# Fused linear attention and squared-ReLU MLP on one core: batch 1's second and batch 2's first matrix multiplication in the plain form, the weights' block sums moved, tail numerators of two batches alternating, and a new table of shifts

## The chip, the core and the metric

The kernel runs on one core of one Trainium2 chip. The core's engines work side by side: TensorE (PE; its weight loads are shown apart as PEld), VectorE (DVE), ScalarE (ACT), GpSimd (POOL) and SyncE (SP), which here only issues transfers. DMA engines move data between HBM and the on-chip memory (SBUF); PE writes to eight PSUM banks. The metric is the time of one execution on the device in microseconds, lower is better. It is given as the median of several runs.

## The reference

Eight batches of eight heads, 576 positions, 64 channels: linear attention with cosine weights, whose output is the input of an MLP with squared ReLU (4608 tokens, width 512, hidden width 2048). Cut to what is computed:

```python
batch, n_heads, seq, head_dim = (8, 8, 576, 64)
n_tokens, d_model, d_ff = (4608, 512, 2048)

theta = np.pi / 2.0 * pos / S
cos_w, sin_w = np.cos(theta), np.sin(theta)
def phi(x, c, s):
    r = np.maximum(x, 0.0)
    return np.concatenate([r * c, r * s], axis=-1)
q_p, k_p = phi(q, cos_w, sin_w), phi(k, cos_w, sin_w)
kv = np.einsum('bhsf,bhsd->bhfd', k_p, v)
z = np.sum(k_p, axis=2)
num = np.einsum('bhsf,bhfd->bhsd', q_p, kv)
den = np.einsum('bhsf,bhf->bhs', q_p, z)[..., None] + 1e-06
x = (num / den).transpose(0, 2, 1, 3).reshape(B * S, H * D)

h = x @ w_in
r = np.maximum(h, 0.0)
g = r * r
out = g @ w_out
```

## The kernel before

**Blocks of tokens.** The 576 positions of a batch are four pieces of 128 and a tail of 64. The MLP works on blocks m of 512 tokens: block m below 8 is the four pieces of batch m, block 8 is the eight tails. Matrices are in bf16, sums in f32.

**Attention of a batch.** k and q are turned into features (`feat`, L321 on ACT and L325 on DVE: ReLU times the cosine or the sine), v is cast beside a column of ones (`att_v`, L343), PE makes kv and z (`att_kv`, L367), and they are copied out (`att_kvz`, L378). The features of q are transposed, from batch 2 on by a DMA (`att_qT`, L391). PE multiplies them with kv (`att_num`, L418), DVE divides by the last column (`att_div`, L436, L439 and L442), and the result x is transposed by a DMA (`att_x`, L459) into xT. Tails of two batches b and b + 1 lie on the two halves of the 128 partitions and go through `att_num` together, batch b's eight matmuls and then batch b + 1's.

**Two forms of a matrix multiplication.** The plain form of the first one (`unit_mm`, L503) takes 64 matmuls with 512 columns, one unit of four for each of 16 blocks of hidden channels; ACT applies the ReLU (L512), DVE squares (`square`, L520). The seven-product form works on a 2 x 2 split of each matrix and needs seven block products for eight, with sums of blocks before and after them:

- first multiplication (`in_product`, L580; planned by `plan_gemm1_7`): four sums of x blocks (`x_sum`, L562), four sums of weight blocks made once (`w1_sum`, L538), and for each of four units seven products of four matmuls with 256 columns. ACT copies one product aside (L976), copies banks into banks to start other sums from them (`seed`, L959) and applies the ReLU to two of four blocks (L596). DVE adds the other two (`in_add`, L603), applies their ReLU (`in_max`, L620) and squares (L520).
- second multiplication (`product`, L748; planned by `plan_gemm2`): eight sums of activation blocks for each m (`g_sum`, L727), eight sums of weight blocks made once (`w2_sum`, L708), seven products of 16 matmuls with 256 columns. ACT seeds (L1027), copies (L1037, L1050), DVE adds (L1033).

Block 0 uses the plain form in both multiplications (`first_mm`, L628, and `first_out`, L653). Block 1's first multiplication is plain; its second, and both of blocks 2 to 8, have seven products. `FIRST_7 = 2` in L1202 is the first block whose first multiplication has seven.

**What sets the order.** After the head of batch 0 all work is put into a planner (`Plan`, L58). Each operation has an engine (or a choice between ACT and DVE, `add_either`), a duration, the tiles it reads and writes, and sometimes a due time. `Plan.order` propagates due times backwards, adds to each operation's due time an entry of the table `SHIFTS` (its key is the operation's number), and lists the operations by a simulated start. `Plan.run` then writes out the instructions in that order: each engine and each queue executes its own in order. Every change of the list of operations renumbers them, and so takes another table. `win[m]` is the stretch of plan time in which the second multiplication of block m, the first of block m + 1 and the attention of batch m + 2 lie side by side.

**The lines around the change.** The weight sums of w_out are entered in L1191 to L1197 with an earliest time (`after=tB + 8`); those of w_in by `plan_w1_sums` in L1233. The activation sums are entered by `plan_gemm1` (L912 to L915) when the plain form makes g, and by `plan_gemm1_7` (L998) otherwise. The result is stored from two buffers `ysb` (`put`, L674).

Of the kernel before, what the change touches and what calls it, by code (L numbers as in the profile page):

```python
# [17 lines left out]


SHIFTS = {  # L20
# [34 lines left out]
}  # L55


# [95 lines left out]
def kernel(  # L153
# [9 lines left out]
    nc = tc.nc  # L163
    P = nc.NUM_PARTITIONS
# [5 lines left out]
    HB = DFF // P  # L170
# [53 lines left out]
    def rows(b):  # L224
        return slice(b % 2 * TAIL, (b % 2 + 1) * TAIL)
# [185 lines left out]

    def att_num(b, j, num=NUM):
        qpT = qpTs[b, j]
        for b2 in (b,) if j < J else (b, b + 1):
            ps = ALL if j < J else rows(b2)
            for hh in range(HH):
                for half in range(2):
                    nc.tensor.matmul(  # L418
                        out=num[half][ps, hh * E1 : (hh + 1) * E1],
                        lhsT=qpT[half][:, hh, ps],  # L420
                        rhs=kvzs[b2][:, half * HH + hh, :],
                        start=True,
                        stop=True,
                    )
# [226 lines left out]
    def first_out(hb):  # L651
        for tt in range(J):
# [5 lines left out]
                stop=(hb == HB - 1),  # L658
            )

    def y_of(m, i):
        if (m, i) not in ys:
            ys[m, i] = home(mlp, [P, 2, DM], "ysb", i, F32)
        return ys[m, i]
# [55 lines left out]
    def g_sum(m, n, h0, h1):  # L720
        in0, in1 = {
            1: (g_block(m, 1, 0), g_block(m, 1, 1)),
            2: (gs_of(m, 1), g_block(m, 0, 0)),
            3: (g_block(m, 0, 0), g_block(m, 1, 0)),
            4: (g_block(m, 0, 1), gs_of(m, 2)),
        }[n]
        nc.vector.tensor_tensor(  # L727
            out=gs_of(m, n)[:, h0:h1, :],
            in0=in0[:, h0:h1, :],
            in1=in1[:, h0:h1, :],  # L730
            op=ALU.add if n == 1 else ALU.subtract,
        )
# [133 lines left out]

    def plan_num(b, j, due):
        r = [where[b, j], ("kvz", b % 3)] + ([("kvz", (b + 1) % 3)] if j == J else [])
        add("PE", 0.27 if j < J else 0.54, lambda: att_num(b, j), r=r, w=[("T",)], due=due)
        add("DVE", 1.05, lambda: att_div(b, j), r=[("T",)], w=[x_key(j)])  # L870

    def plan_x(b, i):
# [29 lines left out]
    def plan_gemm1(m, t, dt, banks, plain=False):  # L902
        order = list(range(HB)) if plain else [hb for h in range(HB2) for hb in (h, h + HB2)]
        for n, hb in enumerate(order):
            plan_unit(m, hb, banks[n % len(banks)], t + n * dt, halves=plain and n < 3)
            u = n // 4
            k = 2 if plain and u == 3 else 4
            if n % k == k - 1:
                a = n % 4 + 1 - k
                add("DVE", 0.06 + 512 * k * 0.00053, lambda u=u, a=a, k=k: square(m, u, plain, a, k),  # L910
                    w=[key for x in order[n + 1 - k : n + 1] for i in range(2) for key in g_keys(m, i, x // HB2, (x % HB2,))])
            if n % 4 == 3:  # L912
                if u >= 2 if plain else u % 2:
                    c = u - 2 if plain else u // 2
                    plan_g_sums(m, 4 * c, 4 * c + 4)  # L915

    def plan_w1_sums(after):
        first, second = [("w1", 0), ("w1", 1)], [("w1", 2), ("w1", 3)]
# [81 lines left out]
    def plan_g_sums(m, h0, h1):  # L1000
        hs = range(h0, h1)
        g = lambda i, j: g_keys(m, i, j, hs)
        s = lambda n: [("gs", n, h) for h in hs]
        dur = 0.06 + 256 * (h1 - h0) * 0.00053
        for n, r, w in (
            (1, g(1, 0) + g(1, 1), s(1)),
            (2, s(1) + g(0, 0), s(2)),
            (3, g(0, 0) + g(1, 0), g(1, 0)),
            (4, g(0, 1) + s(2), s(4)),
        ):  # L1010
            add("DVE", dur, lambda n=n: g_sum(m, n, h0, h1), r=r, w=w)

    def plan_gemm2(m, t, dt):
        hs = range(HB2)
# [170 lines left out]
    for tt in range(J):  # L1185
# [2 lines left out]
            r=[("bank", FIRST_Y[tt])], w=[("y", tt // 2, tt % 2)])  # L1188
        if tt % 2:
            add("SP", 1.5, lambda tt=tt: put(0, tt // 2, nc.sync), r=[("y", tt // 2, 0), ("y", tt // 2, 1)], w=[("out", 0, tt)], lag=3.5)  # L1190
    for n in range(1, 5):  # L1191
        for c in range(2):
            p = {1: 5, 2: 6, 3: 7, 4: 4}[n]
            before = {1: [], 2: [("w2t", 5, c)], 3: [], 4: [("w2t", 6, c)]}[n]
            add("DVE", 0.60, lambda n=n, c=c: w2_sum(n, 4 * c, 4 * c + 4),
                r=before + ([("w2", 2 + c)] if n == 3 else [("w2", c), ("w2", 2 + c)]),
                w=[("w2t", p, c)] + ([("w2", c)] if n == 3 else []), after=tB + 8)  # L1197
    win = {}
    t = tB + 4.0
    dC = 0.98  # L1200
    win[0] = (t, t + 14.0)
    FIRST_7, STRIDE, SHIFT = 2, 2.0, -6.0  # L1202
    if FIRST_7 == 1:
        plan_w1_sums(28.0)
        plan_gemm1_7(1, t, 0.5)
# [11 lines left out]
    for b in range(2, B):  # L1217
# [13 lines left out]
        t0, t1 = win[m - 1]  # L1231
        if m == FIRST_7:
            plan_w1_sums(28.0 if m == 2 else win[m - 2][0])  # L1233
        plan_gemm2(m - 1, t0, (t1 - t0) / 14)
        if m < FIRST_7:
            plan_gemm1(m, t0, (t1 - t0) / HB, (2, 0, 1, 3))
        else:
# [88 lines left out]
```

## Time and profile before

| | us |
|---|---|
| median of 3 runs | 279.09 (278.84 to 279.17) |
| the profiled execution | 279.47 |
| its span (first to last instruction) | 277.7 |
| PE busy in the span | 266.2 (96%) |
| PEld busy | 220.3 (79%) |
| DVE busy | 228.6 (82%) |
| ACT busy | 190.3 (69%) |

The span is what the profile shows; the rest of the profiled execution's time lies around it. PE is not busy only at the beginning (before the first loads have landed), in two stretches between 70 and 100 us, and at the end (the last copies and stores). The chain that ended last runs through PE for 83% of the span, through waits for DMAs for 5%, and through DVE and ACT for 4% each. The granted clock of PE was 0.998.

How to read the views used below: a group's row gives line, engine, operation, what is written and read, count, then busy time and mean duration of one, then the idle time of the engine before these instructions and what ended it. In a row of a timeline or of the chain of waits the first number is the start and the second the length. A matmul's duration includes its way through the array (273 ns for 256 columns), while matmuls follow each other at 109 ns.

### The profile page before, as it was taken

To read this page: it belongs to the slowest core of one execution; us is meant where nothing else is said; L and a number is where in the kernel's file an instruction comes from. 1 tells how busy PE (TensorE), PEld (TensorE's weight loads), DVE (VectorE), ACT (ScalarE), POOL (GpSimd) and SP (SyncE) were. 2 spreads that over 40 slices of the span, in tenths; PEclk is the share of its full clock that TensorE was granted. 3 is DMA by queue.
4 is the path that set the end of the run, shared out by engine and by line. 5 is a ranking of instruction groups with operands and counts; after the bars stand their busy time and mean duration, and the time that the engine had idled before them with its cause. 6 is when DMAs were issued, how large, how long until landed. Compare 5 with 4: busy or idle time off the path is not lost.

```text
span 277.7 us, 6808 instructions
## 1 busy us (share of the span) xinstructions
PE 266.2 (96%) x2755; PEld 220.3 (79%) x2755; DVE 228.6 (82%) x452; ACT 190.3 (69%) x342; POOL 19.2 (7%) x33
## 2 busy tenths in 40 slices
PE   8899999999799979999999999999999999999993
PEld 2478955565589869899899898998988888888882
DVE  1677896889999989899999986999999977697900
ACT  3575862596998989579957996998454563647231
POOL 8427000000000000000000000000000000000023
PEclk9999999999999999999999999999999999999999
DMA  7999999899989999998989599989122200300134
GB/s 211 317 206 289 309 242 316 255 222 346 206 230 240 272 230 190 315 315 151 249 263 306 144 254 243 273 164 218 38 41 84 88 0 2 151 4 0 78 113 113
DMA packets 83470, 53.38 MB, mean 192 GB/s; under 512 B 55888, under 2 KB 79824, under 8 KB 83440
## 3 DMA queue, kind: packets, MB, share of 16 engines
q1 hardware_dynamic: 77312, 42.28, 60.2%
q0 software_dynamic: 6048, 10.62, 16.2%
q8 instruction: 21, 0.34, 0.5%
q10 hardware_dynamic: 80, 0.07, 0.1%
q14 instruction: 9, 0.07, 0.1%
HBM read 36.70 MB, written 9.44 MB: 166 GB/s over the span
## 4 chain that ended last, share of the span: by engine, by line
PE 83%; DMA 5%; DVE 4%; ACT 4%; POOL 1%; issue 1%; POOLq 0%; ACTq 0%; DVEq 0%
PE bank L748 33%; PE bank L580 30%; PE bank L628 4%; PE bank L653 4%; PE bank L503 3%; PE abank L367 3%; PE abank L418 3%; DMA q<-in_q_dram 3%; DMA xT<-x 3%; PE bank L400 1%; ACT qp L321 1%; ACT kp L321 1%; DVE x L442 1%; DVE qp L325 1%; DVE kp L325 1%
## 5 line engine op out<-in xcount | busy, mean ns | idle before, releaser
L748 PEld LDWEIGHTS <-gT 128*128 128x128 bf16 x512 | 49.6, 98 | 6.2
L596 ACT ACTIVATE gT<-bank 128x512 bf16<-128x512 f32 x56 | 33.3, 602 | 26.2 <-PE bank L580 26.1
L580 PE MATMUL bank<-xT,w1sb 128*128 128x256 bf16 x336 | 48.6, 273 | 1.7 <-DMA xT<-x 1.5
L580 PEld LDWEIGHTS <-w1sb 128*128 128x128 bf16 x448 | 43.0, 98 | 7.2 <-DMA xT<-x 1.7
L748 PE MATMUL bank<-w2sb,gT 128*128 128x256 bf16 x384 | 48.0, 273 | 0.0
L603 DVE TENSOR_TENSOR gT<-bank,qpTp 128x512 bf16<-128x512 f32 x56 | 36.3, 684 | 8.6 <-PE bank L580 7.9
L748 PEld LDWEIGHTS <-gs 128*128 128x128 bf16 x384 | 36.8, 98 | 6.7 <-DVE gs L727 2.4
L520 DVE TENSOR_TENSOR gT<-gT 128x2048 bf16<-128x2048 bf16 (+1 forms) x32 | 37.7, 1185 | 1.4 <-ACT gT L596 1.1
L959 ACT COPY bank<-bank 128x512 f32<-128x512 f32 x56 | 31.8, 584 | 5.1 <-PE bank L580 4.3
L580 PEld LDWEIGHTS <-w1t 128*128 128x128 bf16 x336 | 32.0, 98 | 3.6
L748 PE MATMUL bank<-w2t,gs 128*128 128x256 bf16 x256 | 32.4, 273 | 1.9 <-DVE gs L727 1.9
L580 PE MATMUL bank<-qpTp,w1t 128*128 128x256 bf16 x224 | 32.5, 273 | 0.0
L442 DVE TENSOR_TENSOR x<-abank,rden 128x512 bf16<-128x512 f32 x31 | 21.4, 691 | 1.1
L976 ACT COPY qpTp<-bank 128x512 f32<-128x512 f32 x28 | 15.9, 590 | 8.6 <-PE bank L580 7.8
L682 POOL DMA_DIRECT2D out_dram<-ysb x4 | 2.4, 614 | 241.3 <-ACT ysb L1037 238.9
L1033 DVE TENSOR_TENSOR ysb<-bank,y 128x512 f32<-128x512 f32 x16 | 11.0, 687 | 9.3 <-PE bank L748 8.4
L580 PE MATMUL bank<-xT,w1t 128*128 128x256 bf16 x112 | 16.6, 273 | 0.0
L321 ACT ACTIVATE kp<-k,sin_col 128x512 bf16<-128x512 f32 x22 | 15.5, 720 | 1.5 <-DMA k<-in_k_dram 1.5
L580 PE MATMUL bank<-zeros,w1sb 128*128 128x256 bf16 x112 | 16.3, 273 | 0.0
L748 PE MATMUL bank<-w2t,gT 128*128 128x256 bf16 x128 | 16.1, 273 | 0.0
L748 PE MATMUL bank<-w2sb,gs 128*128 128x256 bf16 x128 | 16.1, 273 | 0.0
L628 PE MATMUL bank<-xT,w1sb 128*128 128x256 bf16 (+1 forms) x160 | 15.2, 251 | 0.0
(104 smaller groups left out, 413.7 us busy)
## 6 DMA issues: line engine op xcount, KB each, us to landing
out_dram<-ysb SPq DMA_DIRECT2D x16, 512.0 KB, 3.3
v<-in_v_dram SPq DMA_DIRECT2D x12, 512.0 KB, 5.3
q<-in_q_dram SPq DMA_DIRECT2D x12, 512.0 KB, 6.3
k<-in_k_dram SPq DMA_DIRECT2D x12, 512.0 KB, 6.9
v<-in_v_dram POOLq DMA_DIRECT2D x2, 1024.0 KB, 12.4
w1sb<-in_moe_w_in_dram POOLq DMA_DIRECT2D x4, 512.0 KB, 12.7
w2sb<-in_moe_w_out_dram POOLq DMA_DIRECT2D x4, 512.0 KB, 15.1
k<-in_k_dram SPq DMA_DIRECT2D x1, 1024.0 KB, 5.3
```

Of the source, the lines that this page charges most:

```text
L321: eng.activation(out=dst[ps, :, lo : lo + D], in_=src[ps], func=ACTF.Relu, scale=col[ps])
L442: nc.vector.tensor_tensor(out=x[:, a:z], in0=n4[:, :, :, 0:D].rearrange("p b (k l) d -> p b k l d", l=2), in1=rden[:, a:z] .rearrange("p b ...
L520: nc.vector.tensor_tensor(out=g, in0=g, in1=g, op=ALU.mult)
L580: nc.tensor.matmul(out=bank[to][:, s * W : (s + 1) * W], lhsT=lhs[:, kb, (2 * u + s) * P : (2 * u + s + 1) * P], rhs=rhs[:, kb, :], start= ...
L596: nc.scalar.activation(out=g_pair(m, i, j, u), in_=bank[to][:, :].rearrange("p (s c) -> p s c", s=2), func=ACTF.Relu,)
L603: nc.vector.tensor_tensor(out=g_pair(m, i, j, u), in0=bank[to][:, :].rearrange("p (s c) -> p s c", s=2), in1=in_five(u).rearrange("p (s c) ...
L628: nc.tensor.matmul(out=bank[2 * (s % 2) + i // 2][:, i % 2 * W + c : i % 2 * W + c + step], lhsT=w1sb[:, kb, hb * P : (hb + 1) * P], rhs=x ...
L653: nc.tensor.matmul(out=bank[FIRST_Y[tt]][:, :], lhsT=gT_of(0)[:, hb, tt * P : (tt + 1) * P], rhs=w2sb[:, hb, :], start=(hb == 0), stop=(hb ...
L748: nc.tensor.matmul(out=bank[to][:, s * DM2 : (s + 1) * DM2], lhsT=lhs[:, hb, s * P : (s + 1) * P], rhs=rhs[:, hb, :], start=(fresh and hb ...
L959: add("ACT", psum, lambda: nc.scalar.copy(out=bank[b][:, :], in_=bank[a][:, :]), r=[("bank", a)], w=[("bank", b)])
L976: add("ACT", psum, lambda u=u, Y=Y: nc.scalar.copy(out=in_five(u), in_=bank[Y][:, :]), r=[("bank", Y)], w=five)
L1033: lambda: nc.vector.tensor_tensor(out=y_view(m, i, cc), in0=half_bank(a), in1=five_of(m)[:, :, :], op=ALU.add),
```

## The change

Four things change, besides the table:

1. `FIRST_7` goes from 2 to 3: block 2's first multiplication takes the plain form (`unit_mm`), and the weight sums of w_in are entered for block 3.
2. Block 1's second multiplication takes the plain form, in a new function: 64 matmuls with 512 columns into banks 4 and 5, two groups of 128 tokens at a time, copied out by ACT and DVE. `plan_gemm1` no longer enters activation sums for block 1.
3. The weight sums of w_out are entered behind it, without an earliest time.
4. `att_num` of the tails changes its loops: the two batches' matmuls alternate. The planner's duration for it goes from 0.54 to 0.36.

```diff
 SHIFTS = {
-    40: -2.8, 60: -2, 72: -3.8, 74: -2.4, 78: 4, 92: -1.2, 126: -1.4, 137: 1.2, 145: 7.4, 147: 2.2,
...
+    24: 2.4, 27: 4.4, 38: 2, 45: -2, 70: 2.6, 72: -12, 103: 8.6, 108: -11.2, 111: -8.8, 124: 1.2,
...
 }
...
     def att_num(b, j, num=NUM):
         qpT = qpTs[b, j]
-        for b2 in (b,) if j < J else (b, b + 1):
-            ps = ALL if j < J else rows(b2)
-            for hh in range(HH):
-                for half in range(2):
+        parts = ((b, ALL),) if j < J else ((b, rows(b)), (b + 1, rows(b + 1)))
+        for hh in range(HH):
+            for half in range(2):
+
+                for b2, ps in parts:
                     nc.tensor.matmul(
                         out=num[half][ps, hh * E1 : (hh + 1) * E1],
...
+    LAST_Y = (4, 5)
+
+    def out_pair(m, i, hbs):
+        for hb in hbs:
+            for s_ in range(2):
+                tt = 2 * i + s_
+                nc.tensor.matmul(
+                    out=bank[LAST_Y[s_]][:, :],
+                    lhsT=gT_of(m)[:, hb, tt * P : (tt + 1) * P],
+                    rhs=w2sb[:, hb, :],
+                    start=(hb == 0),
+                    stop=(hb == HB - 1),
+                )
+
+    def pair_copy(m, i, s_, eng):
+        copy = eng.copy if eng is nc.scalar else eng.tensor_copy
+        copy(out=y_of(m, i)[:, s_, :], in_=bank[LAST_Y[s_]][:, :])
...
-        add("PE", 0.27 if j < J else 0.54, lambda: att_num(b, j), r=r, w=[("T",)], due=due)
+        add("PE", 0.27 if j < J else 0.36, lambda: att_num(b, j), r=r, w=[("T",)], due=due)
...
             if n % 4 == 3:
-                if u >= 2 if plain else u % 2:
-                    c = u - 2 if plain else u // 2
-                    plan_g_sums(m, 4 * c, 4 * c + 4)
+                if not plain and u % 2:
+                    plan_g_sums(m, 4 * (u // 2), 4 * (u // 2) + 4)
...
+    def plan_gemm2_plain(m, t, dt):
+        order = list(range(HB))
+        for i in range(2):
+            for n in range(0, HB, 2):
+                hbs = order[n : n + 2]
+                add("PE", 4 * 0.2158, lambda i=i, hbs=hbs: out_pair(m, i, hbs), r=[("w2", hbs[0] // 4)]
+                    + [key for hb in hbs for key in g_keys(m, i, hb // HB2, (hb % HB2,))],
+                    w=[("bank", x) for x in LAST_Y], due=t + (i * HB + n) / 2 * dt, name=f"o{m}.{i}.{n}")
+            for s_ in range(2):
+                e = ("ACT", "DVE")[s_]
+                add(e, cost(e, 512, "psum"), lambda s_=s_, e=e, i=i: pair_copy(m, i, s_, ENG[e]),
+                    r=[("bank", LAST_Y[s_])], w=[("y", i, s_)])
+            add("SP", 1.5, lambda i=i: put(m, i, nc.sync), r=[("y", i, 0), ("y", i, 1)], w=[("out", m, i)], lag=3.5)
...
-    for n in range(1, 5):
-        for c in range(2):
-            p = {1: 5, 2: 6, 3: 7, 4: 4}[n]
...
-                w=[("w2t", p, c)] + ([("w2", c)] if n == 3 else []), after=tB + 8)
+    def plan_w2_sums():
+        for n in range(1, 5):
+            for c in range(2):
+                p = {1: 5, 2: 6, 3: 7, 4: 4}[n]
...
+                    w=[("w2t", p, c)] + ([("w2", c)] if n == 3 else []))
...
-    FIRST_7, STRIDE, SHIFT = 2, 2.0, -6.0
+    FIRST_7, STRIDE, SHIFT = 3, 2.0, -6.0
...
-        plan_gemm2(m - 1, t0, (t1 - t0) / 14)
+        if m == 2:
+            plan_gemm2_plain(1, t0, (t1 - t0) / 16)
+            plan_w2_sums()
+        else:
+            plan_gemm2(m - 1, t0, (t1 - t0) / 14)
```

The rest of `SHIFTS` is replaced in the same way. `win` depends on `FIRST_7` too: the stretch of block 1 becomes 1.6 us of plan time longer.

More of the change, by code (lines that the diff above doesn't have):

```diff
@@ L1190 @@
             add("SP", 1.5, lambda tt=tt: put(0, tt // 2, nc.sync), r=[("y", tt // 2, 0), ("y", tt // 2, 1)], w=[("out", 0, tt)], lag=3.5)
-    for n in range(1, 5):
-        for c in range(2):
-            p = {1: 5, 2: 6, 3: 7, 4: 4}[n]
-            before = {1: [], 2: [("w2t", 5, c)], 3: [], 4: [("w2t", 6, c)]}[n]
-            add("DVE", 0.60, lambda n=n, c=c: w2_sum(n, 4 * c, 4 * c + 4),
-                r=before + ([("w2", 2 + c)] if n == 3 else [("w2", c), ("w2", 2 + c)]),
-                w=[("w2t", p, c)] + ([("w2", c)] if n == 3 else []), after=tB + 8)
+    def plan_w2_sums():
+        for n in range(1, 5):
+            for c in range(2):
+                p = {1: 5, 2: 6, 3: 7, 4: 4}[n]
+                before = {1: [], 2: [("w2t", 5, c)], 3: [], 4: [("w2t", 6, c)]}[n]
+                add("DVE", 0.60, lambda n=n, c=c: w2_sum(n, 4 * c, 4 * c + 4),
+                    r=before + ([("w2", 2 + c)] if n == 3 else [("w2", c), ("w2", 2 + c)]),
+                    w=[("w2t", p, c)] + ([("w2", c)] if n == 3 else []))
     win = {}
```

65 rows, old and new, of the table SHIFTS are left out of this document.

## The prediction

> **What bounds the kernel now.** I read the table of ten-microsecond stretches first, because an average over the whole span hides stages. Its columns are the stretch, then busy time (and instructions) of PE, PEld, DVE, ACT and POOL, granted clock, DMA share, GB/s.
>
> ```profile
> 60.00:70.00 10.00, 10.00 (x77) 5.20 (x76) 8.82 (x19) 6.96 (x14) 0.00 (x0) 1.00 1.06 303
> 70.00:80.00 10.00, 7.87 (x75) 5.78 (x73) 9.90 (x21) 10.00 (x18) 0.00 (x0) 1.00 0.97 230
> 80.00:90.00 10.00, 10.00 (x133) 8.91 (x131) 9.90 (x21) 8.88 (x18) 0.00 (x0) 1.00 1.06 234
> 90.00:100.00 10.00, 8.54 (x91) 7.48 (x89) 9.83 (x20) 9.79 (x18) 0.00 (x0) 1.00 1.14 263
> 130.00:140.00 10.00, 10.00 (x121) 9.02 (x119) 9.96 (x21) 9.49 (x18) 0.00 (x0) 1.00 1.07 212
> ```
>
> Nearly everywhere the matrix engine has no idle time: what counts is the number of matmul columns. The exception is 70 to 100 us, where DVE and ACT are full together and PE stands for 2.13 and 1.46 us. At 130 to 140 DVE is as full and PE loses nothing. So a full DVE alone is no stall; a backlog on it is. That stretch is batch 1's second matmul together with batch 2's first, what the change rewrites. The waits (who waits <- for whom: total, times, longest), the timeline there and the chain that ended last:
>
> ```profile
> PE bank L748 <- DVE gs L727: 1.9, 1, 1.9
> PE bank L580 <- DMA xT<-x: 1.5, 1, 1.5
> ```
>
> ```profile
> 74.55 1.29 DVE L727 TENSOR_TENSOR gs<-gT 128x1024 bf16<-128x1024 bf16 x2
> 75.30 1.21 PE L748 MATMUL bank<-w2t,gs 128*128 128x256 bf16 x8 [1.89 <-DVE gs L727]
> 90.06 0.69 DVE L442 TENSOR_TENSOR x<-abank,rden 128x512 bf16<-128x512 f32 x1
> 91.75 3.36 SPq L459 DMA_TRANSPOSE xT<-x  x1
> ```
>
> ```profile
> 65.00 1.73 PE bank L503 x8
> ...
> 91.75 7.08 DMA xT<-x
> ...
> 259.89 12.24 PE bank L748 x112
> ```
>
> The first wait is for batch 1's activation sums (L727), work that only the seven-product form has. The second is batch 3's x: divided at 90.75 (90.06 + 0.69), its transpose issued at 91.75 behind a load on SP, landed at 98.83, while PE was there at about 97.2. A wait is counted from the modelled end of the last matmul, 273 ns after its start, where matmuls follow at 109 ns; each costs 0.16 us more than its row. With ACT's 0.25 us at 78.9 and a second gs wait (0.16) the stretch loses 1.89 + 1.46 + 0.25 + 3 x 0.16 + 0.16 = 4.2 us.
>
> **The change part by part.** *PE, added.* A seven-product multiplication is 112 matmuls of 256 columns: 12.24 us by the chain's last row. The plain one is 64 of 512; L503's eight take 1.73, so 13.84. Two are exchanged: +3.2 us. In a stretch where PE never waits this goes straight to the end.
>
> *DVE and ACT, removed.* DVE loses for batch 1 eight L727 (0.69 us each) and for batch 2 eight L603 (0.65), four L562 and four L620 (0.42 each): 14.1 us of busy time; two L1033 become two copies of the same length. The planner then hands DVE five more features (0.48) and four fewer casts (0.42). Net 13 us less. ACT: per unit two relus, two seeds and a copy (about 0.59 each), 20 in all, 11.9 us, become 16 relus at 0.61, 9.7; of L1050, L1027 and L1037 five copies become two, 1.8 less; five features fewer and four casts more, 1.1 less: 5 us less. None of this is on PE's path by itself; it is what the 4.2 us waited for.
>
> *Where the backlog goes.* I took both programs' order of instructions, cut it into stretches of 10 us of matmul work from batch 0's first L628, and summed DVE and ACT in each at their back-to-back time (the second L727 above adds 1.29 - 0.69 = 0.60). Before, the sixth stretch (about 71 to 84 us of the trace) holds 13.1 us of DVE and 12.4 of ACT against 10 of PE, and the three after it 10.3, 10.0 and 9.6 of DVE: the backlog reaches 5.1 us and nothing works it off. In the changed program that stretch holds 9.1 and 7.1, the next 4.9 and 4.4, and no stretch more than 10.6 of DVE or 10.1 of ACT. Its largest backlog is 1.9 us; the old program carries 2.1 us at its later peak (about 190 us of the trace) and PE loses nothing there. So I take both waits, and ACT's, as gone: -4.2 us. Bounds: the gs waits must go, their instructions no longer exist (-2.2); the x and seed waits may stay.
>
> *The sums moved.* By the order, three of four L538 weight sums of w_in move from before 42 us to DVE's light stretch around 72 to 77 us, and the fourth stays just behind the last plain matmul that reads its block. Of the eight L708 sums of w_out, four come earlier (among L653's matmuls, where DVE is busy 6.63 of 10 us) and four go to about 106 to 110. DVE executes in order: behind the fourth L538 (1.22) stand a square, the x sums of batch 3 and the gs of batch 2, and PE waits for those. In the 20 us of matmul work from there DVE has 20.5 us of work: cover for all but 0.5 us. SP issues the same number of transfers and transposes; no new queue is passed.
>
> *Tails.* Four times 16 matmuls of 65 columns, two batches one after the other, become alternating pairs on the two halves of the array's columns:
>
> ```profile
> 66.56 0.41 PE L418 MATMUL abank<-kvz,qpT 128*128 128x65 bf16 x8
> 77.31 0.60 PE L418 MATMUL abank<-kvz,qptT 128*64 128x65 bf16 x16
> ```
>
> Eight take 0.41 (a last latency included) and sixteen 0.60: the second eight cost 0.19, or 24 ns each. If pairs ran wholly together, 0.19 would go in each tail, 0.76 in four; if not at all, 0. Near to neither end; the second eight already go faster than the 29 ns of an ordinary one, so some overlap exists: 0.4. The Trainium skill ("TensorE: Matmul & The Clock Gate", section "Wait — 56ns, not 53.3ns?") says that matmul starts never come closer than about 25 ns however small they are. By that rule 64 matmuls could save at most 4 ns each, an estimate of 0.26 us, and the sum would be 0.1 worse; the row's 24 ns already lies at that floor, and single starts of 0 to 7 ns apart occur in the trace.
>
> *What comes late next.* The x transposes. From division to landing they took 3.0 to 8.1 us in this trace, the second of a batch (which the x sums wait for) 5.9 at most; from issue to landing the tile's view says:
>
> ```profile
> DMA to landing us min/median/max: 2.5/4.1/7.2
> ```
>
> In the changed order the division of the second pair stands 7.1 (batch 2), 6.3 (batch 3) and 5.3 us (batch 4) of matmul work ahead of its reader, the first pair 7.7 and more. Most landings fit; the tight ones I price at 0.4 us in all, bounds 0 and 2.6. The program's end (12.24 us of products, then copies and stores) is unchanged.
>
> Sum: +3.2 - 4.2 - 0.4 + 0.4 = -1.0 us. The profiled execution took 279.47 us for a span of 277.7, so 1.8 lie around it, and the median of the runs is 279.09, 0.4 below. The edits touch only the span, so I subtract from the median: **278.1 us**. With 0 for the tails it is 278.5; with all of them and no late landing, 277.3; if head waits go too (0.4 us each at 23.1 and 53.6, where DVE now has less to do), 276.5.
>
> **The rivals.** *Half is given back (same).* The stall only moves: the fourth L538 cannot start before the plain form's last reader, and batch 1's copies out of the banks must wait for batch 0's store to leave that buffer, in the trace 8.24 us at its slowest (issued at 80.13). DVE's 0.5 us without cover and such a store, another 0.6, reach PE at batch 3's product 5 or batch 2's product 5. Then 278.1 + 1.1 = 279.2. For it: 20.5 against 20 us of work. Against it: DVE comes into that stretch without backlog.
>
> *Slower: late transposes.* One mechanism: with plain units PE reaches batches 3 and 4 sooner than their x. If division to landing takes the 8.1 us of batch 3's first pair, not the 3 to 6 of the other second pairs, the three second pairs are late by 8.1 less 7.1, 6.3 and 5.3 less about 0.5 of slack in the x sums: 0.5 + 1.3 + 2.3 = 4.1, less the 0.4 already counted: 278.1 + 3.7 = 281.8; with the two later ones at 7.2 us (0.4 + 1.4, less 0.4) it is 279.5. PE begins to wait at 5.8 us, and from about 7.3 the kernel is slower than before. For it: the DMA engines' share is 1.0 to 1.1 through all these stretches. Against it: only first pairs, behind loads, took over 6.
>
> *It doesn't do what it says.* The tails give nothing, because a change of column half costs what the overlap gains, and the weight sums "later" are half earlier: 278.5.
>
> **How the numbers follow.** Forecast 0.54, given back 0.20, slower 0.20, not as said 0.06; the slower case has a fifth, though no second pair was that late, because two of the six first pairs were. The likeliest alone reaches from 277.3 to 278.6. The range starts at 276.9, where part of the head's waits go as well, and reaches into the slower case, to 280.6; outside lie most of its upper half and little below. About 0.2%, 0.56 us, can be told from no change. The forecast is faster but for a tenth, given back is mostly within, the slower case slower but for its mildest: 0.55 faster, 0.23 same, 0.22 slower.
>
> **What would show it.** Right: between 70 and 100 us PE busy 10 of 10 with DVE under 9.9; no row of PE waiting for gs; L653's kind of matmul (512 columns) 64 more in each of two lines; L418's 16 on qptT in less than 0.60. Wrong: a row of PE or DVE waiting for DMA xT of over 1 us, DVE at 9.9 in 90 to 110 with PE below 9.5, or a wait of DVE for the store of ysb. If PE is full throughout and the time is still above 279, then the two forms' price (3.2) is wrong.

## The result and the profile after

The changed kernel takes 277.5 us (median of 4 runs, 277.15 to 277.98) beside 279.03 for the kernel before on the same chip: a ratio of 0.9947, with a 95% interval of 0.9931 to 0.9963. Run again later beside three experiments it took 277.3 us, 0.9932 (0.9918 to 0.9947). So it is 1.5 to 1.8 us faster; 1.0 was forecast. The profiled execution took 277.98 us for a span of 276.2.

The ten-microsecond stretches of the changed kernel come first; columns as before the change (stretch, then busy time and instructions of PE, PEld, DVE, ACT, POOL, granted clock, DMA share, GB/s).

```profile
70.00:80.00 10.00, 9.95 (x61) 4.54 (x60) 9.90 (x20) 7.94 (x15) 0.00 (x0) 1.00 1.09 231
80.00:90.00 10.00, 9.95 (x101) 5.60 (x101) 4.82 (x13) 6.45 (x12) 0.00 (x0) 1.00 1.00 287
90.00:100.00 10.00, 9.95 (x57) 4.98 (x57) 9.06 (x16) 7.85 (x15) 0.00 (x0) 1.00 1.20 241
```

PE lost 2.13 and 1.46 us here before; now it shows 0.05 in each stretch. These are not waits: the busy table has 2651 matmuls for 2659 weight loads, and each gap of 53 ns follows a pair of starts that is exactly one usual interval of a 512-column matmul (215 ns) too far apart. A matmul record is missing there. DVE, full for 30 us before, has half a stretch to spare between 80 and 90. The list of PE's waits, from its top:

```profile
PE abank L366 <- DVE vext L342: 2.6, 1, 2.6
PE bank L348 <- DVE zeros L243: 1.2, 1, 1.2
PE bank L399 <- ACT qp L320: 0.5, 1, 0.5
PE bank L464 <- DVE x L442: 0.2, 1, 0.2
```

All of the first three lie in the program's first 15 us. The rows for gs (1.9) and for DMA xT (1.5) are gone, and so are the row for L468's xT at 53.6 us and the one for L325's kp at 57.6. The chain that ended last and the timeline of PE show what stands in their place, the plain second multiplication (L667) and a tail:

```profile
70.71 5.99 PE bank L667 x27
```

```profile
78.36 0.44 PE L418 MATMUL abank<-kvz,qptT 128*64 128x65 bf16 x16
```

The first row is from the chain that ended last: 27 matmuls without a break, where PE had stood for gs. The tail of 16 takes 0.44 us where it took 0.60.

To compare kernels whose heads differ by chance, I split each profile like this. The body runs from the first L628 matmul to the end of the last matmul. For each matmul I took the time to the next one's start, less the median of this time for its line and size; what came to 0.23 us or more is summed as waits, and the rest of the body is matmul columns and what hides among them. One kind of gap is left out of the waits: 0.32 or 0.34 us ahead of a matmul of the plain second multiplications (L653 and L667 in the changed kernel) that follows one of a tail, which the profile puts down to issue. The changed kernel's trace has 61 matmuls of L653 and 60 of L667 beside 64 weight loads of each. After the tail at 43 us the next start comes 347 ns later, where the kernel before has 122, and the difference is one 512-column interval: a record is missing there too.

| kernel | body us | waits us | rest us |
|---|---|---|---|
| before | 254.0 | 5.5 | 248.5 |
| changed (both profiles) | 251.6 | 0.7 | 250.9 |
| only the tails (e1) | 253.6 | 5.7 | 247.9 |
| tails, old forms, other order (e7) | 253.8 | 6.1 | 247.7 |
| only the second multiplication plain (e5, e9, e12) | 252.2, 251.6, 251.4 | 2.7, 2.3, 2.1 | 249.5, 249.3, 249.2 |
| only the first one plain (e6) | 251.8 | 2.4 | 249.4 |
| one plain form more (e8) | 253.0 | 0.4 | 252.6 |
| sums put back (e10) | 256.2 | 5.0 | 251.2 |

The changed kernel trades 4.8 us of waits for 2.4 us of rest. Its body is 2.4 us shorter than before, the span only 1.5: in its first profile the first L628 starts at 19.67 us (19.38 in the second), before at 18.99. Over all profiles of kernels with the changed order this start lies at 18.5 to 19.7, with the old order at 18.5 to 19.0, so whether the new table makes the head later or the loads did stays open.

### The profile page after: what moved, and what is told of

The parts are those of the page before. It is cut to its first block, busy times and chain, and to the rows that moved or that the text cites. A ratio compares the mean times of both kernels' runs of the same rounds, so it can differ in the third digit from the quotient of the medians.

```text
span 276.2 us, 6556 instructions
## 1 busy us (share of the span) xinstructions
PE 265.8 (96%) x2651; PEld 210.5 (76%) x2659; DVE 216.5 (78%) x429; ACT 186.4 (67%) x334; POOL 19.3 (7%) x33
## 4 chain that ended last, share of the span: by engine, by line
PE 89%; DMA 3%; ACT 2%; DVE 2%; POOL 1%; issue 1%; POOLq 0%
PE bank L766 31%; PE bank L580 27%; PE bank L503 9%; PE bank L653 5%; PE bank L667 5%; PE bank L628 4%; PE abank L366 3%; PE abank L418 3%; DMA q<-in_q_dram 3%; ACT qp L320 1%; PE bank L399 1%; PE bank L487 1%; ACT gT L638 1%; DVE x L442 1%; PE bank L464 0%
## 5 line engine op out<-in xcount | busy, mean ns | idle before, releaser
L766 PEld LDWEIGHTS <-gT 128*128 128x128 bf16 x448 | 43.5, 98 | 5.1
L766 PE MATMUL bank<-w2sb,gT 128*128 128x256 bf16 x336 | 42.2, 273 | 0.0
L580 PE MATMUL bank<-xT,w1sb 128*128 128x256 bf16 x288 | 41.1, 273 | 0.0
L580 PEld LDWEIGHTS <-w1sb 128*128 128x128 bf16 x384 | 36.9, 98 | 4.5
L596 ACT ACTIVATE gT<-bank 128x512 bf16<-128x512 f32 x48 | 28.8, 605 | 14.4 <-PE bank L580 14.1
L603 DVE TENSOR_TENSOR gT<-bank,qpTp 128x512 bf16<-128x512 f32 x48 | 31.0, 684 | 6.0 <-PE bank L580 5.9
L766 PEld LDWEIGHTS <-gs 128*128 128x128 bf16 x336 | 32.4, 98 | 3.7
L580 PEld LDWEIGHTS <-w1t 128*128 128x128 bf16 x288 | 27.7, 98 | 3.7
L503 PE MATMUL bank<-xT,w1sb 128*128 128x512 bf16 x116 | 27.7, 379 | 0.0
L512 ACT ACTIVATE gT<-bank 128x512 bf16<-128x512 f32 x32 | 18.6, 596 | 10.2 <-PE bank L503 10.1
L503 PEld LDWEIGHTS <-w1sb 128*128 128x128 bf16 x116 | 10.7, 98 | 11.0
L628 PE MATMUL bank<-xT,w1sb 128*128 128x256 bf16 (+1 forms) x160 | 15.4, 251 | 0.1
L436 DVE TENSOR_SCALAR den<-abank 128x8 f32<-128x8 f32 x35 | 5.6, 160 | 12.3 <-PE abank L418 12.3
```

Of the source, the lines that this page charges most:

```text
L503: nc.tensor.matmul(out=out_, lhsT=w1sb[:, kb, hb * P : (hb + 1) * P], rhs=x_block(m, kb), start=(kb == 0), stop=(kb == KB - 1),)
L512: nc.scalar.activation(out=gT_of(m)[:, hb, :], in_=bank[to][:, :], func=ACTF.Relu)
L580: nc.tensor.matmul(out=bank[to][:, s * W : (s + 1) * W], lhsT=lhs[:, kb, (2 * u + s) * P : (2 * u + s + 1) * P], rhs=rhs[:, kb, :], start= ...
L596: nc.scalar.activation(out=g_pair(m, i, j, u), in_=bank[to][:, :].rearrange("p (s c) -> p s c", s=2), func=ACTF.Relu,)
L603: nc.vector.tensor_tensor(out=g_pair(m, i, j, u), in0=bank[to][:, :].rearrange("p (s c) -> p s c", s=2), in1=in_five(u).rearrange("p (s c) ...
L628: nc.tensor.matmul(out=bank[2 * (s % 2) + i // 2][:, i % 2 * W + c : i % 2 * W + c + step], lhsT=w1sb[:, kb, hb * P : (hb + 1) * P], rhs=x ...
```

## The experiments

Ratios are to the kernel before on the same chip in the same session, with their 95% intervals.

**The tails alone (e1).** The kernel before with its old forms and order; only the loop of `att_num` is the new one.

```diff
-        for b2 in (b,) if j < J else (b, b + 1):
-            ps = ALL if j < J else rows(b2)
-            for hh in range(HH):
-                for half in range(2):
+        parts = ((b, ALL),) if j < J else ((b, rows(b)), (b + 1, rows(b + 1)))
+        for hh in range(HH):
+            for half in range(2):
+                for b2, ps in parts:
```

> The kernel before with the tails' matmuls alternating, and nothing else changed (the old table, the old order on every engine). In the trace of the changed kernel the sixteen starts of a tail span about 0.25 us, before 0.40. Theory (PE is the bound wherever a tail stands): 4 x 0.15 = 0.6 us less, 278.4. Rival (the tails' gain is lost in waits for the division that follows, or a switch of column half costs time once other work surrounds it): no change, 279.0. Rival (the tails are the larger part of the whole gain of 1.5 us): 277.9 or less.

278.0 us (277.64 to 279.8), 0.9963 (0.9932 to 0.9993). PE's two long waits, for gs and for xT, have the same rows as before (1.9 and 1.5 us). The first tail in the timeline:

```profile
76.80 0.44 PE L418 MATMUL abank<-kvz,qptT 128*64 128x65 bf16 x16
```

The stalls stay, the tail goes from 0.60 to 0.44. Four of them make 0.6 us, and the rest of the body falls by as much. The body itself is only 0.4 us shorter, because the wait for a seed at 78 us grew by 0.15. The median fell by 1.1, but the interval reaches from 0.2 to 1.9 us.

**The changed kernel with its tails in turn (e2).** The converse edit, in the changed kernel.

> The changed kernel with the tails one batch after the other again, everything else as it is. Theory: 0.6 us more than the changed kernel, 278.1, so that the two plain forms with their table keep 0.9 us. Rival (the forms bring nothing, all of the gain is the tails'): 279.0.

278.17 us, 0.9962 (0.9936 to 0.9987), and the tail again:

```profile
78.07 0.60 PE L417 MATMUL abank<-kvz,qptT 128*64 128x65 bf16 x16
```

The body is 0.7 us longer than the changed kernel's, with the same waits. So alternating gives 0.6 to 0.7 us with either order.

**Short activation sums in the kernel before (e3).**

```diff
     def g_sum(m, n, h0, h1):
+        w = 8 if m == 1 else W
...
-            out=gs_of(m, n)[:, h0:h1, :],
+            out=gs_of(m, n)[:, h0:h1, 0:w],
...
+        for n in (1, 2, 4):
+            nc.gpsimd.memset(gs_of(1, n)[:, :, :], 0.0)
```

> The kernel before with batch 1's activation sums made for 8 of their 256 columns only (the rest of the three buffers is set to zero at the start, by GpSimd, and one block of g keeps its values), so the output of batch 1 is not the reference's. DVE loses about 4.6 us of work around 74 to 95 us; PE does exactly the same matmuls in the same order. Theory (PE's waits between 70 and 100 us are one backlog on DVE): both waits go, 4.2 us, 274.8. Rival (the x wait is the DMA queue's own): the gs waits alone, 2.2 us, 276.8. Rival (the wait moves to the next thing that DVE or ACT owes): under 1 us, 278.0 or more.

Slower: 282.63 us, 1.012 (1.0076 to 1.0165). Most of it I had brought in myself. DVE's and POOL's timelines where the buffers are zeroed:

```profile
27.91 5.23 DVE L325 TENSOR_SCALAR qp<-q,sin_col 128x512 bf16<-128x512 f32 x1
```

```profile
27.54 5.31 POOL L1297 MEMSET gs<- 128x2048 bf16 x3
```

A feature that takes 0.48 us elsewhere takes 5.23 while POOL fills three buffers, and PE then stands for 2.5 us. This run can't be read by its time. What it still tells is the wait in question, in PE's and DVE's timelines:

```profile
77.15 1.05 PE L749 MATMUL bank<-w2t,gs 128*128 128x256 bf16 x8 [1.15 <-DVE gs L728]
```

```profile
74.05 1.22 DVE L520 TENSOR_TENSOR gT<-gT 128x2048 bf16<-128x2048 bf16 x1
75.19 1.22 DVE L538 TENSOR_TENSOR w1sb<-w1sb 128x2048 bf16<-128x2048 bf16 x1
76.32 0.69 DVE L520 TENSOR_TENSOR gT<-gT 128x1024 bf16<-128x1024 bf16 x1
76.92 0.30 DVE L728 TENSOR_TENSOR gs<-gT 128x32 bf16<-128x32 bf16 x2
```

Two sums in 0.30 us where the kernel before took 1.29 shorten PE's wait only from 1.89 to 1.15. The rest is what stands ahead of the sum in DVE's order: squares, and a weight sum of 1.22 us. It is the queue that is late, more than the sum. What the memsets had cost DVE was worked off by then: it begins these sums 1.1 us after PE is ready for them, before 1.3.

The theory itself (one backlog on DVE makes all these waits) failed here. Between 70 and 102 us PE still loses 4.3 us start to start: 0.35 for batch 2's xT, 1.31 for gs, 1.09 for a seed and 1.59 for batch 3's xT. The last one matters most. Its division, its transpose and PE's wait:

```profile
91.48 0.17 DVE L436 TENSOR_SCALAR den<-abank 128x8 f32<-128x8 f32 x1 [0.79 <-PE abank L418]
92.84 4.60 SPq L459 DMA_TRANSPOSE xT<-x  x1
101.21 0.61 PE L580 MATMUL bank<-xT,w1sb 128*128 128x256 bf16 x4 [1.43 <-DMA xT<-x]
```

DVE had been idle, waiting for PE, and the transpose was issued 0.2 us after the division; it landed 8.3 us later. So this wait was not made by DVE's queue, as the run's first rival had said.

**Fewer columns in the plain product (e4).** The changed kernel, `out_pair` on 448 of 512 columns.

```diff
-                    out=bank[LAST_Y[s_]][:, :],
+                    out=bank[LAST_Y[s_]][:, 0:448],
...
-                    rhs=w2sb[:, hb, :],
+                    rhs=w2sb[:, hb, 0:448],
```

> The changed kernel with batch 1's plain second multiplication made for 448 of its 512 columns, so the last 64 columns of batch 1's output are not the reference's. 64 matmuls lose 64 columns each, 27 ns at the 216 ns that 512 take: 1.7 us of matmul work, about what the seven-product form would have saved, and no other engine does less. Theory (nothing but matmul columns sets the time of the changed kernel after the head): 1.7 us less, 275.8. Rival (DVE, ACT or the transfers are just behind PE in this stretch and take over): under 0.8 us less, 276.7 or more.

276.16 us, 0.9905 (0.9874 to 0.9936): 1.3 us below the changed kernel, with an interval of about 1 us on either side. The body is 0.7 us shorter; its rest fell by 1.5, close to the columns taken out, and 0.8 us came back as new small waits, the largest this one:

```profile
PE bank L580 <- ACT bank L976: 0.4, 1, 0.4
```

So columns do set the time, but the cover is thin: a PE that is 1.5 us earlier already meets ACT.

**Half of the change: only batch 1's second multiplication plain (e5).**

```diff
-    FIRST_7, STRIDE, SHIFT = 3, 2.0, -6.0
+    FIRST_7, STRIDE, SHIFT = 2, 2.0, -6.0
```

and a table searched for its own list of operations, as in all that follow except the last two.

> The changed kernel with batch 2's first multiplication back in seven products: only batch 1's second one is plain, with an order worked out anew for this form. PE's columns cost 1.6 us more than before instead of 3.2; DVE loses the eight activation sums of batch 1 (5.5 us) but keeps batch 2's 8.6 us of input sums and bank copies. If the stalls of 70 to 100 us come from DVE's backlog of 5.1 us, 5.5 us less is just enough: waits gone as in the changed kernel, +1.6 - 4.2 - 1.0 (waits at 50 to 59) - 0.6 (tails), so 275 to 276.5 us beside 279.1. If both plain forms are needed for the relief, the x wait and the seeds' waits stay (2 us): 277 or more.

276.79 us, 0.993 (0.9903 to 0.9957), between the times of the theory and of its rival. gs and seed waits are gone; what is left is the row that the slower rival had named:

```profile
PE bank L642 <- DMA xT<-x: 1.2, 2, 0.9
```

**The other half: only batch 2's first multiplication plain (e6).**

```diff
-        if m == 2:
-            plan_gemm2_plain(1, t0, (t1 - t0) / 16)
-            plan_w2_sums()
-        else:
-            plan_gemm2(m - 1, t0, (t1 - t0) / 14)
+        if m == 2:
+            plan_w2_sums()
+        plan_gemm2(m - 1, t0, (t1 - t0) / 14)
```

(The planner enters batch 1's activation sums again as before.)

> The other half alone: batch 2's first multiplication plain, batch 1's second one in seven products with its activation sums, with an order worked out anew for this form. PE +1.6 us, DVE 8.6 us less, ACT 2.2 less. By the backlog theory 8.6 is more than the 5.1 us needed, so PE's waits for gs and xT are gone or under 0.5 together: 275 to 276.5. By the rival that the wait for gs belongs to the form itself (sums that only the seven products have, late however empty DVE is) a wait of PE for gs of 1 us or more stays: 277 to 278.

278.17 us, 0.9972 (0.9957 to 0.9987). In the timeline of PE:

```profile
73.13 1.48 PE L822 MATMUL bank<-w2t,gs 128*128 128x256 bf16 x12 [0.58 <-DVE gs L801]
```

The sums are all there, yet the wait for them fell from 1.89 to 0.58 us when other work left DVE (busy 221.8 us in all, before 228.6). That is below the 1 us that the rival (a wait that belongs to the form) asked for. The order is another one too, though, so it need not be the work alone. The time is above what either theory gave: the body is as short as the changed kernel's (251.8 us), but PE still waits 0.75 for that sum, start to start, 0.8 in all for xT and kp at 53 to 57 and 0.5 for a seed at 267 us.

**The old forms with a new order (e7).** The kernel before with alternating tails and a table searched in the same manner.

> The old forms throughout (both multiplications in seven products), with the alternating tails, and an order of the instructions searched anew in the same manner as for the two kernels with half of the change. If it was DVE's and ACT's work that had to go, no order removes the stalls: 277.7 to 278.6, like the old order with the alternating tails (278.0), with waits of 3 us or more between 70 and 100 us. If the changed kernel owes its gain to its new table of order alone, the waits are gone here too, without the 3.2 us: 274 to 275.5.

279.96 us, 1.0048 (1.0025 to 1.0072): slower than the old order. PE's and DVE's timelines:

```profile
75.28 1.03 PE L642 MATMUL bank<-qpTp,w1t 128*128 128x256 bf16 x8 [1.80 <-DVE qpTp L624]
```

```profile
72.60 0.68 DVE L789 TENSOR_TENSOR gs<-gT 128x1024 bf16<-128x1024 bf16 x1
73.21 1.28 DVE L582 TENSOR_TENSOR gT<-gT 128x1024 bf16<-128x1024 bf16 x2
74.41 0.48 DVE L387 TENSOR_SCALAR kp<-k,cos_col 128x512 bf16<-128x512 f32 x1
74.81 0.41 DVE L624 TENSOR_TENSOR qpTp<-xT 128x512 bf16<-128x512 bf16 x1
```

This order puts the sums of activations early enough, and so the sums of x come late: PE waits 1.80 us for those at 73 and 1.56 at 127. A third new one, 1.4 us for an ACT ReLU, comes at 35 us. So the waits are 6.1 us in all, but only 2.0 of them lie between 70 and 100 us, where the theory had put 3 or more. The wait for batch 3's xT is not among them. Another order chose other victims. One searched order doesn't prove that none exists, but the table alone did not make the gain here.

**One plain form more (e8).**

```diff
-    FIRST_7, STRIDE, SHIFT = 3, 2.0, -6.0
+    FIRST_7, STRIDE, SHIFT = 4, 2.0, -6.0
```

> The changed kernel with one multiplication more in the plain form: batch 3's first one, with an order worked out anew. 64 matmuls of 512 columns for 112 of 256: +1.6 us of PE where it has no wait left to lose. If PE's columns alone set the time now, 1.6 us above the changed kernel: 278.7 to 279.6 (ratio to before 0.999 to 1.002). If DVE's load still costs PE something that the waits don't show, 277.0 to 278.0.

279.08 us, 1.0 (0.9983 to 1.0017). The gain is given back, 1.6 us above the changed kernel, as its first theory said:

```profile
100.00:110.00 10.00, 10.00 (x102) 5.40 (x101) 9.86 (x18) 6.36 (x12) 0.00 (x0) 1.00 0.94 250
```

PE was full there already. ACT gets room that nobody needs (busy 176.5 us in all, in the changed kernel 186.4; DVE 215.4 and 216.5), and 1.6 us of columns go straight to the end: the rest of the body rises by 1.6.

**More room for the transposes (e9, e12).** The kernel e5, each x transpose planned 1.5 us longer, and two separately searched orders.

```diff
-            add("SP", 1.7, lambda: att_x(b, i), r=[x_key(j) for j in js], w=w, lag=1.6 + CARE)
+            add("SP", 1.7, lambda: att_x(b, i), r=[x_key(j) for j in js], w=w, lag=3.1 + CARE)
...
```

> The kernel with only batch 1's second multiplication plain (276.8 us, two waits of PE for DMA xT, 0.26 and 0.94 us, each 0.16 more than its row), with an order worked out anew in which each x transpose is given 1.5 us more between its issue and its first reader. If those two waits were late transposes and nothing else, they go: 1.2 + 0.3 less, 275 to 275.9 us. If the slack only moves the wait to another engine (DVE has to divide earlier), a wait of 0.5 us or more for DVE takes their place: 276.3 to 277.5.

> The same form and the same added 1.5 us, with a second order found from another starting point: it tells how much of a gain belongs to one lucky order. If the form and the slack set the time, within 0.6 us of the other one (275 to 276.2). If the order decides, they lie 1 us or more apart, with a wait in the slower one that the other has not.

279.26 us, 1.0016 (0.9994 to 1.0038), and 277.04 us, 0.9925 (0.991 to 0.9939). PE's waits in e9, then in e12:

```profile
PE bank L546 <- ACT xT L527: 0.7, 1, 0.7
...
PE bank L523 <- DVE x L501: 0.5, 1, 0.5
PE abank L477 <- DMA qpT<-qp: 0.4, 1, 0.4
```

```profile
PE bank L524 <- DVE x L502: 0.9, 1, 0.9
PE bank L547 <- DVE ysb L746: 0.6, 1, 0.6
```

No row for DMA xT is left in either, but start to start PE now waits 2.0 us in e9 (at 54, 55 and 143 us) and 2.1 in e12 (at 53, 54 and 58), where e5 had 0.8 at 52 to 57: the wait moved, as the second theory of e9 said. e9's median lies 1.3 us above its own profiled execution (277.96, the fastest of 12 runs up to 282.04), and e12's five runs lie within 0.3. Why e9 scatters isn't settled. By their medians the two orders of one form lie 2.2 us apart, more than the whole change is worth; in the profiled executions it is 0.7 us of span.

**The sums put back (e10).** The changed kernel in its own order; behind the squares DVE also computes batch 1's eight activation sums, which nothing reads.

```diff
+    def square_and_sums(m, u, plain, a, k):
+        square(m, u, plain, a, k)
+        if plain and m == 1:
+            squared.extend([u] * k)
+            for c in range(2):
+                if u % 2 == c and squared.count(c) == 4 and squared.count(c + 2) == 4:
+                    for p in (1, 2, 3, 4):
+                        g_sum(m, p, 4 * c, 4 * c + 4)
...
-                add("DVE", 0.06 + 512 * k * 0.00053, lambda u=u, a=a, k=k: square(m, u, plain, a, k),
+                add("DVE", 0.06 + 512 * k * 0.00053, lambda u=u, a=a, k=k: square_and_sums(m, u, plain, a, k),
...
```

> The changed kernel, its order kept, with batch 1's eight activation sums put back on DVE behind the squares that they would follow; nothing reads them. PE's work is that of the changed kernel, DVE has 5.5 to 6 us more at about 68 to 80 us, where it is busy 7.25 and 9.90 of 10. If a DVE backlog in itself costs PE time (late gT, x or copies), the backlog rises from 1.9 to about 7 us and PE gets waits for DVE of 1 to 3 us: 278.5 to 280.5. If only the product's wait for its own sums mattered, PE stays full and the time is the changed kernel's, 277.4 to 278.

282.04 us, 1.0117 (1.0092 to 1.0142), 4.7 us above the changed kernel beside it. The stretches, PE's timeline, and DVE's ahead of the second wait:

```profile
70.00:80.00 10.00, 7.94 (x37) 3.35 (x35) 9.79 (x19) 5.99 (x11) 0.00 (x0) 1.00 0.88 186
80.00:90.00 10.00, 8.03 (x92) 4.44 (x92) 6.77 (x15) 5.40 (x10) 0.00 (x0) 1.00 0.77 223
```

```profile
77.43 1.04 PE L678 MATMUL bank<-w2sb,gT 128*128 128x512 bf16 x4 [2.01 <-DVE gT L520]
85.23 1.14 PE L366 MATMUL abank<-vext,kp 128*128 128x65 bf16 x32 [1.97 <-DVE xt L442]
```

```profile
76.69 0.68 DVE L520 TENSOR_TENSOR gT<-gT 128x1024 bf16<-128x1024 bf16 x1
77.41 0.69 DVE L756 TENSOR_TENSOR gs<-gT 128x1024 bf16<-128x1024 bf16 x1
...
79.47 0.68 DVE L756 TENSOR_TENSOR gs<-gT,gs 128x1024 bf16<-128x1024 bf16 x1
```

PE never reads a gs here and yet loses 2 x 2.1 us, first for the last square, which stands behind four sums, then for a division behind four more, some features and two weight sums. This is the clearest run of the study: 5.5 us more on DVE, PE's work and the order untouched, and nearly all of it reaches the end. I had expected 1 to 3 us of waits; it is dearer, because PE meets the late queue twice.

**The changed kernel again (e11).**

> The changed kernel as it is, beside the three above on the same chip: 277.2 to 278.0, ratio 0.993 to 0.9965 to the kernel before. It tells whether the versions with half of the change are faster than the whole.

277.3 us, 0.9932 (0.9918 to 0.9947). The halves e5 (0.993) and e12 (0.9925) overlap with it; no version is shown to beat the change.

## Why the prediction was right, and which terms were off

The forecast was the likeliest case, and it came: faster, 1.5 us where 1.0 was said. Term by term:

- *PE, added, +3.2 us.* Held. The rest of the body grows by 3.0 from the old forms with the new tails (e1) to the changed kernel, and by 1.6 with a third exchange (e8). Singly, the first multiplication costs 1.5 and the second 1.3 to 1.6.
- *DVE and ACT, removed, 13 and 5 us.* Somewhat less: their busy times fell by 12.1 us (228.6 to 216.5) and 3.9 (190.3 to 186.4).
- *The backlog, -4.2 us.* Right in size; in cause shown only in part. The four waits between 70 and 100 us made 4.25 us, and none is left. That DVE's queue makes PE wait is shown by e10, which keeps the changed kernel's order and gives DVE the work back: 4.3 us of waits return in new places. e6 points the same way for gs, in an order of its own. The 1.6 us for batch 3's xT, however, the prediction put down to the same backlog, and e3 speaks against that: there this wait stays, with DVE idle ahead of the division. In the kernel before, the division ended 6.5 us before PE was ready for its x, and landing took 8.1 us from there. In the changed one it ends at 88.69, 8.9 us before its reader (97.55), and landing takes 5.6. Either difference would have been enough to end the wait. So the reason that holds is the one in the prediction's list of distances (7.7 us and more for the first pairs), and that the backlog's term came out whole is partly luck. Whether the plain units or the new table made the distance longer, and why that transpose landed faster, stays open.
- *Tails, -0.4 us.* Mis-sized. They gave 0.6 to 0.7, near the bound of 0.76: 0.40 us of pitch per tail became 0.25. I had drawn the estimate from the 24 ns of the second eight matmuls, taking it that pairs overlap in part; they overlap almost wholly.
- *Late x, +0.4 us.* Not needed. From division to landing the pairs' transposes took 3.1 to 5.8 us, and PE waited for none.
- *The waits at 50 to 59 us.* The step that missed most. The kernel before stands there too, though its description names only the stretches between 70 and 100 us:

```profile
50.00:60.00 10.00, 9.52 (x101) 6.43 (x100) 9.54 (x23) 7.67 (x15) 0.00 (x0) 1.00 0.97 215
```

  Three waits (0.40, 0.33, 0.23) made 1.0 us and left; I had put only the 0.4 at 53.6, together with one at 23.1, into the bound of 276.5, not into the sum. The one at 23 us stayed (0.40), and a new one of 0.30 came at 33.7. What removed the three is not shown: each half of the change, in its own order, keeps 0.8 us of waits there (e5, e6).

With the measured sizes: +3.0 - 4.1 - 1.0 + 0.3 - 0.6 = -2.4 us, which is the body's. (The smallest of the four waits, 0.16, lies under the table's mark and is in its rest.) The head, later by 0.4 to 0.7 us in the profiles, takes some of it back.

The rivals: *half is given back* did not happen, since DVE has 5.2 us of room between 80 and 90 us, ahead of the fourth weight sum (L538, at 96.4 us in the timeline). *Late transposes* did not decide here, but the mechanism is real: PE waits for xT 0.94 us in e5 at 149 us and 1.43 in e3 at 100. *It doesn't do what it says* fell with e1 and e2. Of the signs of being right that were named ahead, all but one came: DVE's 9.90 in 70 to 80 is at the mark of 9.9 and not under it. PE's 9.95 is 10 but for the missing records.

## What to carry to other kernels

When the bounding engine stands only where a helper engine is full, price an algorithm with fewer columns also by what it costs the helper there: here 12 us less on DVE went with 5 us less of waits, and 3 us more on PE was the price. Stop when the waits are used up, since the next exchange (e8) is all price. A wait names the last thing to arrive, not the culprit: ask what stands ahead of it in its engine's order, and check the answer for each wait by itself, since of two neighbouring waits here one was DVE's queue and the other was not. A new order of the old forms (e7) only moved the waits to other rows.

## What the hardware showed that I had not expected

Two matmuls on the two halves of the array's columns start together. The sixteen starts of the changed kernel's tail at 101.54 us follow each other at 4, 49, 3, 33, 3, 26, 3, 29, 4, 26, 3, 32, 4, 26 and 3 ns. In all four tails the two of a pair are 0 to 6 ns apart and pair follows pair at 24 to 33, but for about 49 after the first. The Trainium skill ("TensorE: Matmul & The Clock Gate", section "Wait — 56ns, not 53.3ns?") states a floor of about 25 ns between starts; the section does not speak of matmuls on parts of the array. The floor holds here from pair to pair, not from one half to the other; by it as I read it the four tails could have saved 0.26 us, and they saved 0.6.

A POOL memset can hold up DVE for its whole length. In e3 one feature took 5.23 us in place of 0.48, from 27.91 to 33.14, beside three memsets from 27.54 to 32.85; DVE got no turn between them. The Trainium skill ("SBUF — State Buffer", section "SBUF: two separate sides") says that the two engines share a pair of ports, which some of DVE's instructions need and which one instruction holds exclusively, the other blocking fully. This trace agrees, and adds that three in a row count as one.
